# One product of the first layer made by seven inner products for pairs of units, in the last two of four sequences

## The chip, the cores and the metric

The kernel runs on one core of one Trainium2 chip. The metric is the time of one execution on the device in microseconds (us), as a median of three runs.

## The reference

Four sequences of 768 tokens go through an attention block with eight heads of 64, in which a query sees only the keys of its own cluster, and then through a feed-forward block. The change is in the feed-forward block alone, which is, for the attention's output `x` of 768 x 512 a sequence:

```python
mu = np.mean(x, axis=-1, keepdims=True)
var = np.mean((x - mu) ** 2, axis=-1, keepdims=True)
xn = (x - mu) / np.sqrt(var + 1e-06) * g_ln
ch = np.maximum(xn @ w_ch1, 0.0) @ w_ch2      # 512 x 2048, 2048 x 512
return (x + ch).astype(np.float32)
```

Everything is float32.

## The kernel before

**Stages.** The attention of all sequences comes first (0 to about 316 us of the span). Then each sequence b = 0 to 3 has a first layer (`xn @ w_ch1` and the ReLU) and a second layer. From sequence 1 on the second layer is `deep_layer`. The span's stages are, roughly: first layer of sequence 0 to 388 us and its second layer to 466; then a first layer and a second layer each for sequence 1 (466 to 604), 2 (604 to 740) and 3 (740 to 881).

**The first layer.** It is one step of a Strassen scheme in Winograd's form: the weight `w1` is taken as 2 x 2 blocks (two halves of the 2048 hidden rows, two halves of the 512 inputs), the tokens as 2 x 2 blocks (two halves of the inputs, two halves of the tokens), and seven block products replace eight. The block products are cut into eight units j = 0 to 7 of 128 hidden rows of each half (`NFH` = 8). `first_layer(b, j, part)` makes product `part` of unit j: `product` (L853) issues two matmuls, one for each 128 inputs of a half, with 128 x 128 weights and 384 columns (`HC`), into one PSUM bank. Products 1, 6, 7 and 4 add up in one bank `x`, 5 and 3 in a bank `z`; product 2 (`w1_block(0, 1, j)` with `x_block(b, 1, 0)`) has a bank `y` of its own. Six banks serve x and z in turn, two serve y and small things. In between, the contents of x are kept: ScalarE copies them (`kept`, L881) as p1 after product 1, u2 after 6, u3 after 7; VectorE adds p1 to y, u2 and u3 to z (`add_relu`, L886), and ScalarE takes the ReLU in place (`relu`, L894) or straight from x (L922). A product that adds onto x waits until the copy of what was in it is done.

The operands that aren't given blocks are sums by VectorE: four of the tokens a sequence (`x_sum`, L645) and four of the weights a unit (`w1_sums`, L661, made one unit ahead).

**The second layer.** `deep_layer` is two steps of the same scheme: 7 x 7 products, each of four matmuls with 192 columns (`QC`), `deep_product` (L1150), with VectorE's and ScalarE's adds and copies of 192 columns (L1163, L1165). Its weights, or sums of them, come from DRAM through a ring of ten places (`ring_load`, L1092); its other operands are sums of the hidden tiles: `outer_sums` (L1103 to L1106, a unit at a time, while the first layer runs), `outer_late`, `inner_sums` (L1124, L1126, quarters) and `inner_late` (L1131, L1133). The first product's quarter sums for chunks 0 to 2 of four stand in the last unit of the first layer, those of the last chunk after it.

**What sets the order.** In these stages the order of the instructions on TensorE, VectorE, ScalarE and SP queue is the order in which the Python code issues them; each engine takes its own in that order and waits by semaphores. `first_units(b, j)` issues a unit: products 1, 2, 4 (of unit j - 1), 6, 3 (of unit j - 1), 5, 7, with ReLUs, the next unit's weight sums and the outer sums of unit j - 1 in fixed places. `unit_end(b, j)` follows each unit: on ScalarE the row norm of one tile of the next sequence's tokens (`norm_rows`, L573 to L575, whose rows SP loads, L560), jobs that the second layer before put off with `later` (an add of the input, `add_rest`, L1203, and a transposition to the output's form, `turn`, L1209; `None` ends what one unit end takes), and `leave(4)`, four of the output DMAs (L1223) that a transposition left behind, eight for each.

For sequences 2 and 3 the first layer's start is interleaved with the end of the second layer before: product 1 of unit 0 stands before the last step of `deep_layer`, and then come products 2, 6, 5, 7 of unit 0.

Of the kernel before, what the change touches and what calls it, by code (L numbers as in the profile page):

```python
# [23 lines left out]
def kernel(  # L24
# [1100 lines left out]
        if 1 in which:  # L1125
            nc.vector.tensor_tensor(a21[:, cs], a11[:, cs], a21[:, cs], ALU.subtract)  # L1126

    def inner_late(st, m, way):
        q = st["q", m]
        if way == 1:  # L1130
            nc.vector.tensor_tensor(q[6], q[5], q[1], ALU.subtract)  # L1131
        else:
            nc.vector.tensor_tensor(q[3], q[2], q[6], ALU.subtract)  # L1133

# [86 lines left out]
    def leave(n, queues=(nc.sync,)):  # L1221
        for i, (to, y) in enumerate(leaving[:n]):
            queues[i % len(queues)].dma_start(out=to, in_=y)  # L1223
        del leaving[:n]

    pending = []

# [3 lines left out]
    def deep_layer(b, more, st):  # L1231

        done = {}

        def ahead_of(m):
            p = st[m] = {}
            onto = {2: 1, 3: 5}.get(m)
            p["add"] = done.get(onto)
            p["to"] = done[m] = done[onto] if onto else unit(f"m{m}")
            if m == ORDER[-1] and not more:  # L1240
                p["ends"] = {}

        def sum_onto(i, j):
            nc.vector.tensor_tensor(done[i], done[i], done[j], ALU.add)

        def last_part(o, way):

            part = {2: (0, 0), 7: (1, 1), 4: (1, 0), 3: (0, 1)}.get(way)
            if part is None:
                return  # L1250
            r, j = part
            queues = (nc.sync, nc.scalar, nc.gpsimd, nc.gpsimd) if way == 7 else (nc.sync, nc.scalar)
            if way in (4, 3):

# [12 lines left out]
            y = unit("y_end")[:, 0, :QC]  # L1267
            nc.vector.transpose(y, o[:, j].rearrange("p (t a r) -> p t a r", a=2, r=Q)[:, :, r])
            to = out[b].rearrange("(a r t) m -> a (r t) m", r=Q, t=NT)[r]
            for i in range(P // Q):  # L1270
                m = MH + j * P + i * Q
                queues[i % len(queues)].dma_start(  # L1272
                    out=to[:, m : m + Q], in_=y[i * Q : (i + 1) * Q].rearrange("r (t f) -> r t f", f=Q)
                )

        def between():
            first_layer(b, NFH - 1, 3)
            relu(len(summed))
# [12 lines left out]

        def out_of(r, k, m):
            return lambda: turn(b, r, k, done[m])

        def onto(i, j):
            return lambda: sum_onto(i, j)

        jobs = {
            (4, 1): [lambda: first_layer(b, NFH - 1, 4)],
            (4, 2): [between],  # L1300
            (4, 5): [lambda: rest_load(b, 0)],
            (4, 3): [rest(1, 0, 4)],
            (7, 6): [s4(0)], (7, 4): [s4(1)], (7, 3): [s4(2)], (1, 6): [s4(3)],
            (1, 4): [onto(4, 7)], (6, 3): [onto(6, 1)],
            (5, 4): [onto(4, 6)], (5, 3): [onto(5, 6)], (2, 6): [onto(7, 5)],
        }
        for i, m in enumerate(ORDER[1:]):
            for n, way in enumerate((5, 7)):
                jobs.setdefault((ORDER[i], way), []).append(lambda m=m, n=n: inner_sums(st, m, (n,)))
        if more:  # L1310
            for at, (i, c) in (
                ((4, 4), (0, 0)), ((7, 5), (0, 1)), ((1, 3), (0, 2)), ((6, 6), (0, 3)),
                ((6, 5), (1, 0)), ((6, 4), (1, 1)), ((5, 6), (1, 2)), ((5, 5), (1, 3)),
            ):
                jobs.setdefault(at, []).append(norm(i, c))
            for at, c in (((4, 7), 1), ((7, 2), 2), ((7, 3), 3)):
                jobs.setdefault(at, []).append(lambda c=c: norm_load(b + 1, c))
            jobs[2, 4] = [out_of(1, 0, 4)]
            jobs[2, 3] = [rest(0, 0, 2), lambda: rest_load(b, 1)]
            jobs[3, 6] = [lambda: x_sum(b + 1, 1)]  # L1320
            jobs[3, 5] = [lambda: w1_sums(b + 1, 0, (0, 1))]
            jobs[3, 7] = [lambda: first_layer(b + 1, 0, 1)]
            jobs[3, 4] = [lambda: x_sum(b + 1, 2)]
            later(
                rest(1, 1, 7), out_of(1, 1, 7), out_of(0, 0, 2), None,
                rest(0, 1, 3), out_of(0, 1, 3), None,
            )
        else:
            jobs[7, 2] = [lambda: rest_load(b, 1)]
            jobs[1, 3] = [rest(1, 1, 7)]  # L1330
            jobs[5, 6] = [rest(0, 0, 1), onto(4, 6)]
            del jobs[5, 4]
            jobs[2, 5].append(rest(0, 1, 5))
            jobs[2, 1] = [out_of(1, 0, 4)]
            jobs[2, 7].append(out_of(1, 1, 7))
            jobs[2, 3] = [out_of(0, 0, 2)]

        for m, way in STEPS:
            if way == 1:
                ahead_of(m)  # L1340
            deep_product(st, m, way)
            ring_load(b)
            leave(2 if more else 4, (nc.sync,) if more else (nc.sync, nc.scalar))
            if way == 1:
                inner_late(st, m, way)
            for job in jobs.get((m, way), ()):
                job()
            if way == 2:
                inner_late(st, m, way)
            if m == 3 and not more:  # L1350
                for part in {4: (), 3: (4, 3)}.get(way, (way,)):
                    last_part(done[m], part)
        leave(len(leaving))
        places[1, 1], places["e"] = places["e"], places[1, 1]

    deep = {}

    def first_units(b, j):

        chunks = within.pop(j, []) if b == 0 else []  # L1360
        for part, ahead in ((1, 0), (2, 0), (4, 1), (6, 0), (3, 1), (5, 0), (7, 0)):
            if chunks and part in (1, 3):
                split_weight(chunks[0])
            if j >= ahead:
                first_layer(b, j - ahead, part)
            if part in (4, 6, 3):
                relu(1)
            if chunks and part in (2, 3):
                m = chunks.pop(0)
                join_weight(m)  # L1370
                load_weight(m + RAWS)

            if part == 5 and j + 1 < NFH:
                w1_sums(b, j + 1)
            if part == 5 and b and j:
                outer_sums(j - 1, b > 1 or j > 4)
                if j + 1 == NFH:
                    inner_sums(deep[b], ORDER[0], cs=slice(0, NQH - 1))

    with tc.manual_schedule(engines=order):  # L1380
        first_layer(0, 0, 1)
# [79 lines left out]
    with tc.manual_schedule(engines=order | {mybir.EngineType.SP}):  # L1461
# [4 lines left out]
        def unit_end(b, j):  # L1466

            if b + 1 < B:
                if j == 0:
                    rows_load(b + 1, 1)  # L1470
                if j < NT:
                    norm_rows(b + 1, j)
            if b == 1:
                leave(4)
# [19 lines left out]
                norm_stats(b + 1)  # L1494
            if b + 1 < B and j + 2 == NFH:
                norm_stat_rows(b + 1)
            leave(4)
            if b == 1:
                if turning and j % 2 == 0:
                    columns_turn(row, lambda out, in_: leaving.append((out, in_)))  # L1500
# [7 lines left out]
        for b in range(1, B):  # L1508
            deep[b] = {}
            if b + 1 < B:  # L1510
                rows_load(b + 1, 0)
            if b == 1:
                w2_back(1)
                first_units(b, 0)
            else:
                first_layer(b, 0, 2)
                first_layer(b, 0, 6)
                relu(1)
                w1_sums(b, 0, (2, 3))
                x_sum(b, 3)  # L1520
                first_layer(b, 0, 5)
                first_layer(b, 0, 7)
                x_sum(b, 4)
                w1_sums(b, 1)
            unit_end(b, 0)
            for j in range(1, NFH):
                first_units(b, j)
                unit_end(b, j)
            relu(len(summed))
            inner_sums(deep[b], ORDER[0], cs=slice(NQH - 1, NQH))  # L1530
            if b == 1:
                first.close()
                units = pool("units", 1)
# [233 lines left out]
```

## Time and profile before

| | |
|---|---|
| median of three runs | 883.36 us (883.06 to 883.62) |
| the profiled execution | 882.89 us, span 881.1 us, granted TensorE clock 0.998 |
| TensorE matmul busy | 871.2 us, 99% of the span |
| VectorE busy | 703.9 us, 80% |
| ScalarE busy | 403.3 us, 46% |
| first layer of sequence 2, from 604 to 671 us | TensorE 67.0 us, VectorE 38.7, ScalarE 33.7 |
| first layer of sequence 3, from 740 to 807 us | TensorE 67.0 us, VectorE 38.7, ScalarE 24.2 |

The span is the time from the first to the last instruction of the profiled execution; its own time has about 1.8 us more. A float32 matmul leaves two records on TensorE. Records overlap, since matmuls are pipelined, so that a matmul's cost is read from the distance between starts and not from its duration. A group of instructions is named by its line in the kernel, its engine and its operation, then output and inputs by the names of the tiles.

### The profile page before, as it was taken

The numbers are of one execution on the slowest core, as the hardware profiler recorded it, in microseconds if no ns is written. First come the engines' busy times: TensorE is split into PE (matmuls) and PEld (weight loads), VectorE is DVE, ScalarE is ACT, GpSimd is POOL, SyncE is SP. The second block draws the span as 40 slices with busy tenths as digits, with TensorE's granted clock in tenths as the row PEclk, the third lists the DMA queues.
The fourth block names the chain that finished last, engine by engine and source line by source line (L and its number), as shares of the span: only waits on it lengthen the run. The fifth ranks groups of instructions, "written<-read, shape, count | busy, mean of one in ns | idle before, by whom it ended". The sixth has DMA issues, their size and how long they took to land.

```text
span 881.1 us, 13202 instructions
## 1 busy us (share of the span) xinstructions
PE 871.2 (99%) x4648; PEld 575.4 (65%) x4648; DVE 703.9 (80%) x1148; ACT 403.3 (46%) x742; POOL 77.9 (9%) x143
## 2 busy tenths in 40 slices
PE   9999999999999999999999999999999999999996
PEld 5444444444444445568886558997557997556996
DVE  6899999999999888959677787997546887645775
ACT  6777788888888823330004542102552101333110
POOL 1011221222222212110000000000000000000000
PEclk9999999999999999999999999999999999999999
DMA  7777899999986328876675888854236862511875
GB/s 155 145 128 128 147 178 186 206 194 203 186 184 188 100 83 221 239 183 234 186 191 162 240 282 295 295 164 99 55 75 202 280 199 54 102 71 34 272 196 113
DMA packets 250426, 151.01 MB, mean 171 GB/s; under 512 B 192096, under 2 KB 207984, under 8 KB 249328
## 3 DMA queue, kind: packets, MB, share of 16 engines
q1 hardware_dynamic: 219328, 130.80, 56.1%
q0 software_dynamic: 7776, 15.03, 8.9%
q10 hardware_dynamic: 23248, 4.25, 2.7%
q8 instruction: 39, 0.64, 0.3%
q14 instruction: 35, 0.29, 0.1%
HBM read 108.40 MB, written 33.25 MB: 161 GB/s over the span
## 4 chain that ended last, share of the span: by engine, by line
PE 99%; DVE 0%; ACT 0%; issue 0%; ACTq 0%
PE x_ps L855 19%; PE s_ps L401 18%; PE a_ps L413 14%; PE x_ps L1150 12%; PE z_ps L855 9%; PE z_ps L1150 6%; PE x_ps L963 5%; PE y_ps L855 5%; PE y_ps L1150 3%; PE z_ps L963 2%; PE sim_ps L320 1%; PE den_ps L469 1%; PE y_ps L963 1%; PE idle_ps L700 0%; PE qk_ps L303 0%
## 5 line engine op out<-in xcount | busy, mean ns | idle before, releaser
L401 PE MATMUL s_ps<-t,t 64*128 64x384 f32 x768 | 154.8, 483 | 0.0
L401 PEld LDWEIGHTS s_ps<-t,t 64*128 64x128 f32 x768 | 68.0, 187 | 39.0 <-issue 38.3
L1150 PE MATMUL x_ps<-lower,w 128*128 128x192 f32 x448 | 80.8, 326 | 0.4 <-DVE u L1165 0.4
L1150 PEld LDWEIGHTS x_ps<-lower,w 128*128 128x128 f32 x448 | 74.2, 190 | 2.1 <-DVE u L1165 0.7
L886 DVE TENSOR_TENSOR lower<-z_ps,u 128x384 f32<-128x384 f32 x56 | 30.9, 553 | 52.7 <-PE z_ps L855 42.6
L396 ACT ACTIVATE e<-s_ps 128x768 f32<-128x768 f32 x84 | 67.1, 812 | 7.0 <-PE s_ps L401 6.4
L396 ACT ACTIVATE w<-s_ps 128x768 f32<-128x768 f32 x80 | 64.4, 812 | 8.3 <-PE s_ps L401 7.7
L894 ACT ACTIVATE lower<-lower 128x384 f32<-128x384 f32 x88 | 44.9, 521 | 43.7 <-DVE lower L886 43.7
L401 PE MATMUL s_ps<-mask,mask 64*128 64x384 bf16 x384 | 62.8, 323 | 1.0 <-ACT e L396 0.6
L881 ACT COPY u<-x_ps 128x384 f32<-128x384 f32 x64 | 30.6, 478 | 68.1 <-PE x_ps L855 68.0
L413 PE MATMUL a_ps<-e,v_sb 128*64 128x384 f32 x336 | 57.6, 488 | 0.0
L413 PE MATMUL a_ps<-w,v_sb 128*64 128x384 f32 x320 | 55.2, 488 | 0.0
L881 ACT COPY p<-x_ps 128x384 f32<-128x384 f32 x32 | 15.1, 472 | 83.7 <-PE x_ps L855 82.1
L855 PE MATMUL x_ps<-xn,w 128*128 128x384 f32 x128 | 46.6, 487 | 0.0
L855 PE MATMUL x_ps<-xn,ws 128*128 128x384 f32 x128 | 46.6, 487 | 0.0
L855 PE MATMUL x_ps<-xt,ws 128*128 128x384 f32 x128 | 46.6, 487 | 0.0
L855 PE MATMUL x_ps<-xt,w 128*128 128x384 f32 x128 | 46.5, 486 | 0.0
L855 PE MATMUL z_ps<-xn,ws 128*128 128x384 f32 x128 | 46.5, 486 | 0.0
L855 PE MATMUL y_ps<-xn,w 128*128 128x384 f32 x128 | 46.5, 486 | 0.0
L855 PE MATMUL z_ps<-xt,ws 128*128 128x384 f32 x128 | 46.5, 486 | 0.0
L413 PEld LDWEIGHTS a_ps<-e,v_sb 128*64 128x64 f32 x336 | 23.5, 137 | 31.8 <-issue 29.3
L1272 POOL DMA_DIRECT2D out_dram<-y_end x2 | 1.2, 597 | 485.4 <-DMA out_dram<-y 485.4
(232 smaller groups left out, 1678.6 us busy)
## 6 DMA issues: line engine op xcount, KB each, us to landing
w<-w_d SPq DMA_DIRECT2D x84, 256.0 KB, 3.1
raw<-in_moe_w_ch_dram SPq DMA_DIRECT2D x32, 512.0 KB, 4.8
w<-w_t SPq DMA_DIRECT2D x36, 256.0 KB, 5.1
w<-tb POOLq DMA_DIRECT2D x32, 256.0 KB, 5.6
w_d<-wt SPq DMA_DIRECT2D x7, 1024.0 KB, 5.6
w<-w_all SPq DMA_DIRECT2D x27, 256.0 KB, 2.9
v_sb<-in_v_dram SPq DMA_DIRECT2D x32, 192.0 KB, 4.4
xr<-x_d SPq DMA_DIRECT2D x24, 256.0 KB, 3.0
```

The source lines that it names most:

```text
L320: nc.tensor.matmul(sim[r : r + Q, :HC], cT[:, pr, :, :].rearrange("p j c -> p (j c)"), prepared[n][side][:, g * HC : (g + 1) * HC], start= ...
L396: nc.scalar.activation(e, s[:, :, :HC], AF.Exp, scale=SCALE)
L401: nc.tensor.matmul(s[:, j, :HC], of_keys[:, keys], of_queries[:, o : o + HC], start=part == first, stop=part != first, skip_group_check=True,)
L413: nc.tensor.matmul(acc[j * D : (j + 1) * D, :HC], loaded[n]["v"][:, j, c, :], e[:, j, :], start=(c == 0), stop=(c == NT - 1),)
L469: nc.tensor.matmul(den[r : r + Q, :HC], ones, sums[n, g][h][:, j, :], start=h == 0, stop=h == parts - 1, tile_position=(0, r), skip_group_ ...
L855: nc.tensor.matmul(bank[:, :HC], lhs[:, c, :], rhs[:, c], start=first and c == 0, stop=c == NDH - 1, skip_group_check=True,)
L881: nc.scalar.copy(t, bank[:, :HC])
L886: nc.vector.tensor_tensor(h, bank[:, :HC], other, ALU.add)
L894: nc.scalar.activation(h, h, AF.Relu)
L963: nc.tensor.matmul(bank[:, :MH].rearrange("p (h f) -> p h f", h=2), hidden[lhs + (c,)][:, tt * P : (tt + 1) * P], rhs[:, :, c], start=firs ...
L1150: nc.tensor.matmul(bank, w[:, c, :], a[:, c], start=way in (1, 2, 5) and c == 0, stop=c == NQH - 1, skip_group_check=True,)
L1272: queues[i % len(queues)].dma_start(out=to[:, m : m + Q], in_=y[i * Q : (i + 1) * Q].rearrange("r (t f) -> r t f", f=Q))
```

## The change

For sequences b >= `PAIRED` (2 and 3) product 2 is no longer issued. For each pair of units (j, j + 1, j even) the four block products that it stood for (two units, two groups of 128 inputs) are taken as a 2 x 2 block product with halves of 192 columns, and made by seven inner products of one matmul each (128 x 128 weights, 192 columns), by the same scheme. Inner products 1, 6, 7, 4 add up in one x bank, 5 and 3 in a z bank, 2 has a y bank. After 1, 6, 7 and 4 VectorE reads the bank and adds the unit's p1 (a half of it), then adds what it kept to y and z: seven adds of 192 columns a pair, in place of two of 384. The operands are four sums of tokens a sequence (`inner_x`, L1240 of the changed kernel) and four sums of 128 x 128 weights a pair (`inner_w`, L1254); the matmul is at L1272, the adds at L1276 to L1284. The ReLU of the tiles is as before.

The order changes with it. In these sequences a unit issues products 1, 5, 4, 6, 3, 7, with the inner products of a pair spread over its two units, and product 6 follows product 1 of unit 0 at the start. The row norm moves from the unit's end to after product 1, the outer sums to other places in the unit, the put-off jobs by one unit end, eight output DMAs leave at a unit's end instead of four, and the first quarter sums of the second layer all stand after the last unit, their late sum in two pieces (`inner_late` with `cs`).

```diff
+    def inner_x(b):
+        x = x_block(b, 1, 0)
+        (b11, b12), (b21, b22) = [[x[:, k, h * NT // 2 : (h + 1) * NT // 2] for h in range(2)] for k in range(2)]
...
+        for o, x, y in ((t1, b12, b11), (t2, b22, t1), (t3, b22, b12), (t4, b21, t2)):
+            nc.vector.tensor_tensor(o, x, y, ALU.subtract)
+        inner[b, "x"] = {1: b11, 2: b21, 3: b22, 4: t4, 5: t1, 6: t2, 7: t3}
+
+    def inner_w(b, j):
+        (a11, a12), (a21, a22) = [[w1_block(0, 1, j + i)[:, k] for k in range(2)] for i in range(2)]
...
+        for o, x, op, y in (
+            (s1, a21, ALU.add, a22), (s2, s1, ALU.subtract, a11),
+            (s3, a11, ALU.subtract, a21), (s4, a12, ALU.subtract, s2),
+        ):
+            nc.vector.tensor_tensor(o, x, y, op)
+        inner[b, "w"] = {1: a11, 2: a12, 3: s4, 4: a22, 5: s1, 6: s2, 7: s3}
+
+    def inner_products(b, j, ways):
+        a, x, kept = inner[b, "w"], inner[b, "x"], inner[b, "kept"]
+        half = [slice(h * QC, (h + 1) * QC) for h in range(2)]
+        p1, u2, u3 = [kept[:, i * QC : (i + 1) * QC] for i in range(3)]
+        add = {1: (0, 0), 6: (0, 1), 7: (1, 1), 4: (1, 0)}
...
+        for way in ways:
+            name = {2: "y", 5: "z", 3: "z"}.get(way, "x")
+            if way in (1, 2, 5):
+                inner[b, "in", name] = ps(name + "_ps")
+            bank = inner[b, "in", name][:, :QC]
+            nc.tensor.matmul(bank, a[way], x[way], start=way in (1, 2, 5), stop=True, skip_group_check=True)
+            if way in add:
+                r, h = add[way]
+                o = {1: p1, 6: u2, 7: u3}.get(way)
+                nc.vector.tensor_tensor(
+                    to(r, h) if o is None else o, bank, sets[b, j + r]["p1"][:, half[h]], ALU.add
+                )
+            if way == 2:
+                nc.vector.tensor_tensor(to(0, 0), bank, p1, ALU.add)
+            elif way == 7:
+                nc.vector.tensor_tensor(to(1, 1), inner[b, "in", "z"][:, :QC], u3, ALU.add)
+            elif way == 3:
+                nc.vector.tensor_tensor(to(0, 1), bank, u2, ALU.add)
+                summed.extend(hidden_tile(0, j + i) for i in range(2))
...
-            jobs[3, 6] = [lambda: x_sum(b + 1, 1)]
+            jobs[3, 6] = [lambda: x_sum(b + 1, 1), lambda: x_sum(b + 1, 2)]
...
-            jobs[3, 4] = [lambda: x_sum(b + 1, 2)]
             later(
-                rest(1, 1, 7), out_of(1, 1, 7), out_of(0, 0, 2), None,
+                *[None] * (b + 1 >= PAIRED), rest(1, 1, 7), out_of(1, 1, 7), out_of(0, 0, 2), None, *[None] * (b + 1 >= PAIRED),
...
-            if way == 1:
+            if way == 1 and b >= PAIRED and m == ORDER[0]:
+                for cs in (slice(0, NQH - 1), slice(NQH - 1, NQH)):
+                    if cs.start:
+                        inner_sums(st, m, cs=cs)
+                    inner_late(st, m, way, cs)
+            elif way == 1:
                 inner_late(st, m, way)
...
-        for part, ahead in ((1, 0), (2, 0), (4, 1), (6, 0), (3, 1), (5, 0), (7, 0)):
+        parts = ((1, 0), (2, 0), (4, 1), (6, 0), (3, 1), (5, 0), (7, 0))
+        sums_after, inner_at = 5, {}
+        if b >= PAIRED:
+            parts = ((1, 0), (5, 0), (4, 1), (6, 0), (3, 1), (7, 0))
+            sums_after, inner_at = 3, {5: (7,), 6: (4, 3)} if j % 2 else {6: (1, 2), 7: (6, 5)}
+            if j == 1:
+                inner_at = {1: (1, 2), 6: (6, 5), 3: (7,), 7: (4, 3)}
+        for part, ahead in parts:
...
+            if part in inner_at:
+                inner_products(b, j - j % 2, inner_at[part])
+                relu(len(summed))
+            if inner_at and part == 1 and j % 2 == 0:
+                if j == 2:
+                    outer_sums(0, True)
+                inner_w(b, j)
+            if inner_at and part == 1 and b + 1 < B and j < NT:
+                norm_rows(b + 1, j)
...
-            if part == 5 and j + 1 < NFH:
+            if part == sums_after and j + 1 < NFH:
                 w1_sums(b, j + 1)
...
+            if inner_at and part == 7 and j % 2 == 0:
+                outer_sums(j - 1, True)
...
-            leave(4)
+            leave(8 if b >= PAIRED else 4)
...
             else:
-                first_layer(b, 0, 2)
                 first_layer(b, 0, 6)
-                relu(1)
                 w1_sums(b, 0, (2, 3))
                 x_sum(b, 3)
                 first_layer(b, 0, 5)
+                x_sum(b, 4)
                 first_layer(b, 0, 7)
-                x_sum(b, 4)
                 w1_sums(b, 1)
+                inner_x(b)
+                inner_w(b, 0)
...
-            inner_sums(deep[b], ORDER[0], cs=slice(NQH - 1, NQH))
+            if b >= PAIRED:
+                inner_sums(deep[b], ORDER[0], cs=slice(0, NQH - 1))
+            else:
+                inner_sums(deep[b], ORDER[0], cs=slice(NQH - 1, NQH))
```

More of the change, by code (lines that the diff above doesn't have):

```diff
@@ L1126, in inner_sums, with inner_late @@
             nc.vector.tensor_tensor(a21[:, cs], a11[:, cs], a21[:, cs], ALU.subtract)
-    def inner_late(st, m, way):
+    def inner_late(st, m, way, cs=slice(0, NQH)):
         q = st["q", m]
         if way == 1:
-            nc.vector.tensor_tensor(q[6], q[5], q[1], ALU.subtract)
+            nc.vector.tensor_tensor(q[6][:, cs], q[5][:, cs], q[1][:, cs], ALU.subtract)
         else:
@@ L1224, in leave @@
         del leaving[:n]
+    PAIRED = 2
+    inner = {}
+    def inner_x(b):
+        x = x_block(b, 1, 0)
+        (b11, b12), (b21, b22) = [[x[:, k, h * NT // 2 : (h + 1) * NT // 2] for h in range(2)] for k in range(2)]
+        t1, t2, t3, t4 = [
+            unit_part.rearrange("p (t q) -> p t q", q=2 * Q)
+            for unit_part in unit("xi").rearrange("p a c -> p (a c)").rearrange("p (i c) -> i p c", i=4)
+        ]
+        for o, x, y in ((t1, b12, b11), (t2, b22, t1), (t3, b22, b12), (t4, b21, t2)):
+            nc.vector.tensor_tensor(o, x, y, ALU.subtract)
+        inner[b, "x"] = {1: b11, 2: b21, 3: b22, 4: t4, 5: t1, 6: t2, 7: t3}
@@ new lines, in inner_w @@
+    def inner_w(b, j):
+        (a11, a12), (a21, a22) = [[w1_block(0, 1, j + i)[:, k] for k in range(2)] for i in range(2)]
+        if (b, "s") not in inner:
+            inner[b, "s"] = unit("wi").rearrange("p a c -> p (a c)")
+            inner[b, "kept"] = unit("pi").rearrange("p a c -> p (a c)")
+        s1, s2, s3, s4 = [inner[b, "s"][:, i * P : (i + 1) * P] for i in range(4)]
+        for o, x, op, y in (
[4 more added lines that the diff above has]
+        inner[b, "w"] = {1: a11, 2: a12, 3: s4, 4: a22, 5: s1, 6: s2, 7: s3}
@@ new lines, in inner_products, with to @@
+    def inner_products(b, j, ways):
[3 more added lines that the diff above has]
+        add = {1: (0, 0), 6: (0, 1), 7: (1, 1), 4: (1, 0)}
+        def to(r, h):
+            return hidden_tile(0, j + r)[:, half[h]]
+        for way in ways:
[17 more added lines that the diff above has]
+                summed.extend(hidden_tile(0, j + i) for i in range(2))
@@ L1371, in first_units @@
                 load_weight(m + RAWS)
-            if part == 5 and j + 1 < NFH:
+            if part == sums_after and j + 1 < NFH:
                 w1_sums(b, j + 1)
-            if part == 5 and b and j:
-                outer_sums(j - 1, b > 1 or j > 4)
-                if j + 1 == NFH:
+            if part == sums_after and b and j:
+                if not inner_at or j % 2 and j > 1:
+                    outer_sums(j - 1, b > 1 or j > 4)
+                if j + 1 == NFH and not inner_at:
                     inner_sums(deep[b], ORDER[0], cs=slice(0, NQH - 1))
+            if inner_at and part == 7 and j % 2 == 0:
+                outer_sums(j - 1, True)
     with tc.manual_schedule(engines=order):
@@ L1468, in unit_end @@
             if b + 1 < B:
-                if j == 0:
+                if j == 0 and b < PAIRED:
                     rows_load(b + 1, 1)
-                if j < NT:
+                if j < NT and (b < PAIRED or j == 0):
                     norm_rows(b + 1, j)
@@ L1511 @@
                 rows_load(b + 1, 0)
+                if b >= PAIRED:
+                    rows_load(b + 1, 1)
             if b == 1:
@@ L1529 @@
             relu(len(summed))
-            inner_sums(deep[b], ORDER[0], cs=slice(NQH - 1, NQH))
+            if b >= PAIRED:
+                inner_sums(deep[b], ORDER[0], cs=slice(0, NQH - 1))
+            else:
+                inner_sums(deep[b], ORDER[0], cs=slice(NQH - 1, NQH))
             if b == 1:
```

## The prediction

> **What bounds the kernel now.** I read the page's busy table and the 40 slices first, then the tensor engine's timeline in the first layer of sequence 2 (604 to 671 us), then the vector engine's and the groups by form.
>
> ```profile
> span 881.1 us, 13202 instructions
> PE 871.2 (99%) x4648; PEld 575.4 (65%) x4648; DVE 703.9 (80%) x1148; ACT 403.3 (46%) x742; POOL 77.9 (9%) x143
> PE   9999999999999999999999999999999999999996
> ```
>
> TensorE is busy in every slice but the last, so a microsecond of tensor work taken out is a microsecond of time, as long as nothing else makes it wait. The timeline gives the price of a product, as the distance between starts (durations overlap):
>
> ```profile
> 664.17 1.45 PE L855 MATMUL x_ps<-xt,w 128*128 128x384 f32 x4
> 665.46 1.45 PE L855 MATMUL x_ps<-xt,ws 128*128 128x384 f32 x4
> 666.75 1.45 PE L855 MATMUL z_ps<-xn,ws 128*128 128x384 f32 x4
> 668.04 1.45 PE L855 MATMUL z_ps<-xt,ws 128*128 128x384 f32 x4
> ...
> 677.10 1.46 PE L1150 MATMUL z_ps<-qs,w 128*128 128x192 f32 x8
> 678.40 1.46 PE L1150 MATMUL x_ps<-fifth,w 128*128 128x192 f32 x8
> ```
>
> A product of the first layer, two matmuls of 384 columns (four records, each float32 matmul leaves two), takes 1.29 us: 0.645 a matmul. A product of the second layer is four matmuls of 192 columns, each with weights of its own, and takes 1.30 us: 0.325 a matmul, all but exactly half. A unit of seven products takes 9.03 us (616.33 to 625.36).
>
> Vector work in one whole unit of that stage, and the spare time:
>
> ```profile
> 643.40:652.40 9.00, 9.00 (x29) 5.32 (x28) 4.48 (x11) 4.81 (x12) 0.00 (x0) 1.00 0.56 140
> ```
>
> The columns after the length are PE, PEld, DVE, ACT, POOL busy, the clock (full), DMA share and GB/s. VectorE works 4.48 us of 9.00, ScalarE 4.81.
>
> **What it removes and adds on TensorE.** In sequences 2 and 3 product 2 goes from all 16 units: 16 x 1.29 = 20.64 us. Each of 8 pairs of units gets seven single matmuls of 192 columns: 56 x 0.325 = 18.20 us. The changed program's instruction order shows just this, and no other tensor work changed. Saved: 2.44 us, 0.305 a pair. The nearest row for the new matmuls is the second layer's: the same width, and there too every matmul has new weights and every product changes bank. I take it. From above I bound a matmul by its LDWEIGHTS record (190 ns, for two passes 0.38 us): 56 x 0.38 = 21.28, a loss of 0.64 us. From below by half of a 384-column one (0.3225): a gain of 2.58.
>
> A rule speaks against cutting products this small: the Trainium skill, "TensorE: Matmul & The Clock Gate", section "Back-to-back issue gap", says that in a stream of weight load and matmul both set the spacing, and gives about 81 ns at 128 columns where the streaming alone would be 56. By that ratio, as an estimate from the page, a new matmul would cost 0.47 us and the change would lose about 5.7 us. The 1.30 us row above shows no such addition at 192 columns, so the row stands.
>
> **What it adds on VectorE, and whether that stays hidden.** The groups by form (time in all, mean ns of one), and then three starts from VectorE's timeline:
>
> ```profile
> L886 DVE TENSOR_TENSOR lower<-y_ps,p 128x384 f32<-128x384 f32 x32 | 17.4, 544 | 14.2 <-PE y_ps L855 14.1 <-ACT p L881 0.2
> L1165 DVE TENSOR_TENSOR u<-x_ps,m 128x192 f32<-128x192 f32 x12 | 4.2, 352 | 4.1 <-PE x_ps L1150 4.1
> L1124 DVE TENSOR_TENSOR qs<-lower 128x192 f32<-128x192 f32 x2 | 0.7, 358 | 1.2 <-ACT lower L894 1.2
> ```
>
> ```profile
> 625.27 0.40 DVE L661 TENSOR_TENSOR ws<-w 128x256 f32<-128x256 f32 x1
> 625.71 0.42 DVE L661 TENSOR_TENSOR ws<-ws,w 128x256 f32<-128x256 f32 x1
> 626.05 0.42 DVE L661 TENSOR_TENSOR ws<-w 128x256 f32<-128x256 f32 x1
> ```
>
> Per pair two adds of 384 go (2 x 0.544 = 1.09 us); seven of 192 come (7 x 0.352 = 2.46) and four of 128 columns on weights. No row has 128 columns: the slope from 256 (0.418) to 192 (0.358) puts it at 0.30; bounds 0.2 and 0.358; I take 0.29. That is +2.53 us a pair, and 4 x 0.358 a sequence for the tokens: 23 us in all. With it VectorE works 2 x 4.48 + 2.53 = 11.5 of the 17.76 us of a pair. The sum fits; what matters is that four of the new matmuls must wait until VectorE has read the bank they write, or has made their operand. So I go through the queues by hand. Rules from rows: a reader starts 0.20 us after its product (product 3 ends at 666.75 + 1.29 = 668.04, the add starts at 668.24); an instruction that reads the one ahead starts 0.03 after its end (625.27 + 0.40, 625.71), another one 0.08 before it (625.71 + 0.42, 626.05).
>
> The first pair is the tightest. Zero is the end of product 7 of unit 0. TensorE: product 1 of unit 1 to 1.29, inner 1 and 2 to 1.94, product 5 from 1.94, 4 from 3.23, 6 from 4.52, inner 6 at 5.81 and 5, product 3 of unit 0 from 6.46, inner 7 at 7.75, product 7 from 8.08, inner 4 at 9.37 and 3 at 9.69. VectorE: ScalarE has copied u3 at 0.68, the add starts at 0.71, the first weight sum ends at 1.18 + 0.42 = 1.60 (needed at 1.94: room 0.34). Three more weight sums, four token sums and four inner weight sums bring the read of inner 1 to 4.83, done at 5.18 (needed at 5.81: room 0.63). Product 3 ends at 7.75; its add starts at 7.95, the read of inner 7 at 8.42, done at 8.77 (needed at 9.37: room 0.60); the add that frees z ends at 9.15 (needed at 9.69: room 0.54). So no wait. That small rooms do cost nothing, the trace shows: the sum that product 7 of unit 0 reads ended at 604.83 + 0.95 = 605.78, and the product started on schedule at 606.00.
>
> In later pairs 2.6 to 2.9 us of other products lie between an inner product and the one waiting for its read, so rooms are larger. The worst queue there is the jobs that `later` puts off (an add of 0.95 and two transpositions of 0.95) ahead of pair 2. On the same axis unit 1's adds keep VectorE until 11.55, the jobs until 14.32, three outer sums (1.53 in the trace) until 15.85, four inner weight sums until 16.80; the read of inner 1 is done at 17.15, needed at 18.41: room 1.26.
>
> What is moved: product 6 of unit 0 takes product 2's place, so token sum 2 is made under the last products of the second layer: it follows sum 1 (596.12 + 0.95), and the weight sums behind it end near 598.85, 3.3 us before product 6, now at 602.13. The read behind these, at 598.44 in the trace, slips to about 598.8 and ends at 599.16; TensorE's step at 599.53 waits for it: room 0.37. At the entry of the second layer the quarter sums now stand behind the last unit: counted from the start of its first product, the outer sums of unit 6 take VectorE until 1.56, the last unit's add until 2.03, two quarter sums until 3.6, the late sum of three chunks ends at 4.40, needed at 5.18; the fourth chunk's ends at 5.46, needed at 6.16. Rooms 0.7 to 0.8. ScalarE's row norm (five records, 1.80 us from 607.87 to 609.67) moves from the unit's end behind the copy of p1: on the axis above from 1.97 to 3.8, and ScalarE is next needed for product 4's output at 4.72. Eight output DMAs leave at a unit's end where four did; behind them on SP queue the row loads (asked two units ahead of ScalarE's use) and the ring's weight loads (wanted only in the second layer). I cost all this at nothing; were the cover gone, each missed joint would cost its overrun in each of two sequences.
>
> **The sum.** The profiled execution took 882.89 us (span 881.1): 882.89 - 2.44 = 880.45. The three runs' median, 883.36, lies 0.47 above it, so I forecast 883.36 - 2.44 = 880.92, 880.9 us. That is 0.28%; no change, to a measurement of this kernel, is within 0.2% (1.77 us).
>
> **Rivals.**
> First, slower: a wait of VectorE gets in the way of the reads. The trace has one in this very stage:
>
> ```profile
> 623.46 0.98 DVE L1209 STREAM_TRANSPOSE y<-m 128x768 f32<-128x768 f32 x1 [4.61 <-DMA out_dram<-y]
> ```
>
> There the third transposition waits for a buffer that leaves in two portions of four DMAs at two unit ends; TensorE's unit took 9.03 us all the same. If one of 4.61 us stood ahead of pair 2's read, all above the room of 1.26 would stop TensorE: 3.35 us a sequence, 6.7 in two, 887.6 us. Slower by over 0.2% it is once it costs 2.44 + 1.77 = 4.21 us, 2.1 a sequence: from a stall of 1.26 + 2.1 = 3.4 us on. Against it: the first two transpositions now come a unit later, long after their buffers' DMAs, and eight DMAs leave at once (8 x 0.65 us to issue, about 2.1 to land), a unit and more before the third.
>
> Second, the same: single 192-column matmuls between 384-column ones don't hide their weight loads; at 0.38 us each 883.36 + 0.64 = 884.0. For it, they stand alone or in twos; against it, the 1.30 us.
>
> Third, a partial gain: VectorE's small sums or latencies are slightly longer and the first pair misses some of four rooms by 0.2 to 0.5 us each, 0.7 to 1.6 us over two sequences: 881.6 to 882.5. That the product isn't replaced is excluded by the instruction order.
>
> **How the numbers follow.** Forecast 0.79, first rival 0.06, second 0.06, partial gain 0.09 (of which a third still over 0.2% faster). Faster 0.79 + 0.03 = 0.82; same 0.12; slower 0.06. Range: below, the 2.58 us gain and the spread of three runs (0.3) give 880.4, rounded to 880.3; above, the partial gain's end, 882.5. Outside lie the two costly rivals, 0.12.
>
> **What would show it.** Right: a pair of units takes 17.76 us between starts of product 1, against 18.06; the seven inner matmuls show 0.33 us between starts; TensorE has no idle before them; VectorE busy rises by some 23 us. Wrong: idle at inner 4, 3 or 6 put down to VectorE (first or third rival), or starts of 0.38 us and more (second).

## The result and the profile after

The changed kernel takes 880.0 us, median of seven runs (879.66 to 881.18), against 883.24 us for the kernel before in seven runs beside it (882.47 to 883.86): a ratio of 0.9965, 95% interval [0.9954, 0.9977]. It is faster, as forecast, by more than the 0.2% that counts as a difference here. But 880.0 lies 0.3 us under the low end of the range, so the range failed.

The busy table of the changed kernel and TensorE's 40 slices:

```profile
span 878.1 us, 13380 instructions
PE 867.9 (99%) x4696; PEld 581.1 (66%) x4696; DVE 723.4 (82%) x1230; ACT 404.5 (46%) x742; POOL 78.0 (9%) x143
PE   8999999999999999999999999999999999999996
```

TensorE is still busy throughout (8 tenths in the first slice, where it had 9), with 3.3 us less of work recorded; VectorE works 19.5 us more. The timeline of TensorE over unit 1 of sequence 2, in which the first pair's inner products stand (start, record's length, line, tiles):

```profile
605.71 1.45 PE L855 MATMUL x_ps<-xn,w 128*128 128x384 f32 x4
607.00 0.49 PE L1272 MATMUL x_ps<-xn,w 128*128 128x192 f32 x2
607.32 0.49 PE L1272 MATMUL y_ps<-xn,w 128*128 128x192 f32 x2
607.65 1.45 PE L855 MATMUL z_ps<-xt,ws 128*128 128x384 f32 x4
...
610.23 1.45 PE L855 MATMUL x_ps<-xt,ws 128*128 128x384 f32 x4
611.52 0.49 PE L1272 MATMUL x_ps<-xi,wi 128*128 128x192 f32 x2
611.84 0.49 PE L1272 MATMUL z_ps<-xi,wi 128*128 128x192 f32 x2
612.17 1.45 PE L855 MATMUL z_ps<-xn,ws 128*128 128x384 f32 x4
...
615.40 0.49 PE L1272 MATMUL z_ps<-xn,wi 128*128 128x192 f32 x2
615.72 1.45 PE L855 MATMUL x_ps<-xn,w 128*128 128x384 f32 x4
```

Read the starts: 607.00, 607.32, 607.65 are 0.32 to 0.33 us apart, the price taken from the second layer. No line carries a wait in brackets, and from product 1 of unit 1 (605.71) to that of unit 2 (615.72) it is 10.01 us, what the hand count on its axis gave. From there to product 1 of unit 4 (633.48) a pair of units takes 17.76 us, the time forecast. The groups by form say the same for all matmuls of a kind (busy in all, mean ns of one, then idle just before them):

```profile
L1272 PE MATMUL x_ps<-xi,wi 128*128 128x192 f32 x32 | 7.8, 326 | 0.0
L1276 DVE TENSOR_TENSOR pi<-x_ps,p 128x192 f32<-128x192 f32 x24 | 8.5, 353 | 8.8 <-PE x_ps L1272 8.7
L1254 DVE TENSOR_TENSOR wi<-w 128x128 f32<-128x128 f32 x16 | 4.4, 277 | 0.0
```

TensorE idles 0.0 us before the inner products; it is VectorE that waits for them (8.7 us), not the other way round.

Where did the 3 us between the two spans come from? The traces can be cut at fixed points: product 1 of the first unit of sequence 2, the first product of each second layer, and the last transposition on TensorE, before and then after:

```profile
874.40 0.40 PE L1259 MATMUL turned<-ident,end 128*96 128x128 f32 x2 [0.46 <-ACT y_end L1261]
```

```profile
871.66 0.39 PE L1320 MATMUL turned<-ident,end 128*96 128x128 f32 x2 [0.46 <-ACT y_end L1322]
```

Between the first and the last of these points lies all code that the change touches, apart from token sum 2 and the transfers.

| us | before | after |
|---|---|---|
| start of sequence 2's product 1 | 598.24 | 597.95 |
| from there to its second layer | 72.38 | 71.15 |
| sequence 3, product 1 to second layer | 72.26 | 71.04 |
| product 1 of sequence 2 to the last transposition | 276.16 | 273.71 |
| from there to the end of the span | 6.70 | 6.44 |

The two first layers gain 1.23 and 1.22 us, 2.45 in all, against 2.44 forecast. The other 0.55 us (0.29 ahead of the first point, 0.26 behind the last) are in code that the change leaves alone. Part of it can be seen at the start of sequence 0's first layer, before and then after:

```profile
319.89 1.45 PE L855 MATMUL y_ps<-xn,w 128*128 128x384 f32 x4
321.30 1.56 PE L855 MATMUL x_ps<-xt,ws 128*128 128x384 f32 x4
322.70 1.45 PE L855 MATMUL z_ps<-xt,ws 128*128 128x384 f32 x4
```

```profile
319.82 1.45 PE L855 MATMUL y_ps<-xn,w 128*128 128x384 f32 x4
321.11 1.45 PE L855 MATMUL x_ps<-xt,ws 128*128 128x384 f32 x4
322.40 1.45 PE L855 MATMUL z_ps<-xt,ws 128*128 128x384 f32 x4
```

The same three products start 1.41 and 1.40 us apart in the one execution and 1.29 apart in the other. That raised the question whether this belongs to the change or to the execution, which the first two runs settle.

### The profile page after: what moved, and what is told of

It is laid out like the page before. It is cut to its first block, busy times and chain, and to the rows that moved or that the text cites. A ratio compares the mean times of both kernels' runs of the same rounds, so it can differ in the third digit from the quotient of the medians.

```text
span 878.1 us, 13380 instructions
## 1 busy us (share of the span) xinstructions
PE 867.9 (99%) x4696; PEld 581.1 (66%) x4696; DVE 723.4 (82%) x1230; ACT 404.5 (46%) x742; POOL 78.0 (9%) x143
## 4 chain that ended last, share of the span: by engine, by line
PE 97%; DMA 1%; SPq 0%; DVE 0%; ACT 0%; ACTq 0%; issue 0%; DVEq 0%
PE x_ps L855 19%; PE s_ps L401 17%; PE a_ps L413 14%; PE x_ps L1150 12%; PE z_ps L855 9%; PE z_ps L1150 6%; PE x_ps L963 5%; PE y_ps L1150 3%; PE z_ps L963 2%; PE y_ps L855 2%; PE den_ps L469 1%; PE sim_ps L320 1%; PE x_ps L1272 1%; PE y_ps L963 1%; PE z_ps L1272 1%; SPq L92 0%
## 5 line engine op out<-in xcount | busy, mean ns | idle before, releaser
L413 PEld LDWEIGHTS a_ps<-w,v_sb 128*64 128x64 f32 x320 | 22.4, 137 | 30.4 <-issue 27.6
```

The lines of the kernel that those rows point to most:

```text
L413: nc.tensor.matmul(acc[j * D : (j + 1) * D, :HC], loaded[n]["v"][:, j, c, :], e[:, j, :], start=(c == 0), stop=(c == NT - 1),)
```

## The experiments

All share the kernel before on their chip as the yardstick. The theory: TensorE sets the pace; the change is worth the columns it takes out (2.44 us), nothing else in it is worth or costs anything, as long as VectorE's reads come within their rooms; what the first comparison showed beyond it is scatter. The rivals: the moved transfers and the new order bring the rest; or the inner products cost more than counted and something else brings more.

### The same two kernels again

No edit to either kernel.

> The kernel before once more, unchanged. It asks how far two executions of one program differ outside the changed stretch, since the changed kernel's profile gained 2.45 us between product 1 of sequence 2 and the last transposition on TensorE, and 0.55 us elsewhere (0.29 by 390 us of the span, 0.26 after TensorE's last instruction). If the 0.55 us is scatter: the time is that of the kernel before within 0.2%, and this profile differs from the first profile of before by 0.2 to 0.4 us in those two places as well. If it belongs to the change: this profile repeats the first one within 0.1 us in both places (TensorE reaches the first second-layer product of sequence 0 near 389.5 us, and 6.7 us lie behind its last instruction).

> The changed kernel once more. If the gain is TensorE's work alone: 2.45 us, a ratio of 0.9972, and the sequences 2 and 3 give 1.23 us each in the profile. If something else in the change brings 0.6 us: 3.0 to 3.2 us, 0.9965, and the places outside the changed stretch are again 0.2 to 0.3 us shorter than in the profiles of before.

Measured: the kernel before once more 883.82 us against 883.6 (29 runs, 882.61 to 884.96), ratio 1.0004 [0.9995, 1.0013]. The changed kernel 880.88 us (880.43 to 881.84), ratio 0.9972 [0.9961, 0.9984]; the forecast was 880.9 and 2.44/883.36 makes a ratio of 0.9972.

Between the fixed points the second pair of traces repeats the first to a hundredth: 276.16 us for the kernel before, 273.71 for the changed one. Outside them it does not: sequence 2's product 1 starts at 599.30 and 598.82, the tail is 6.94 and 6.87. One program differs from itself by 1.06 us there (598.24 and 599.30, the kernel before), and the two executions of the changed kernel by 1.30 us in both places together (spans of 878.1 and 879.4). So the 2.45 us belong to the change, and the 0.55 us of the first pair to those two executions. What makes the executions differ stays open.

### The new order alone

```diff
-                inner_products(b, j - j % 2, inner_at[part])
+                even = j - j % 2
+                for way, unit_of in ((1, even), (7, even + 1)):
+                    if way in inner_at[part]:
+                        first_layer(b, unit_of, 2)
...
```

Product 2 of each unit stands where inner product 1 or 7 of the pair stood, and the inner sums are gone; order, row norms, put-off jobs, eight DMAs at a unit's end and the split late sum stay as in the changed kernel.

> The changed order (products, row norms, outer sums, put-off jobs, DMAs in eights, quarter sums) with product 2 kept whole, two matmuls of 384 columns a unit, and no inner sums or products. If only the inner products gain: the time of the kernel before, 0 within 0.3 us, no wait on TensorE in sequences 2 and 3. If the order or the DMAs bring part of the gain: 0.5 to 0.8 us less than before, ratio 0.9991 to 0.9994.

Measured: 883.27 us, ratio 0.9997 [0.9988, 1.0006]; 276.15 us between the fixed points, against 276.16. The new order and the moved transfers bring nothing and cost nothing. The whole gain is the inner products'.

### In one sequence only

```diff
-    PAIRED = 2
+    PAIRED = 3
...
```

Sequence 2 starts with products 1, 2, 6, 5, 7 of unit 0 again, without inner sums.

> The inner products and their order in sequence 3 alone. If the gain is TensorE's work: half of it, 1.22 us (0.9986), with 0 in sequence 2 and 1.22 in sequence 3 of the profile. If a fixed part comes from the tail, which this kernel shares: 1.22 + 0.3 to 0.6 = 1.5 to 1.8 us.

Measured: 882.05 us, ratio 0.9986 [0.9977, 0.9995], half of the gain within the interval. The trace is sharper: sequence 2's first layer takes 72.37 us, as before, and sequence 3's 71.04, as after. The gain is local to the layer in which the product is replaced, 1.22 us each.

### Filling a small room

After `inner_w(b, 0)`, ahead of the read of inner product 1, VectorE makes two sums of 128 x 768 that nothing uses.

```diff
+                for _ in range(2):
+                    spare = xpool.tile([P, S], F32, tag="row", name="spare", bufs=2)
+                    nc.vector.tensor_tensor(spare, normed[b][0][:, 0], normed[b][0][:, 0], ALU.add)
```

> The changed kernel with two further sums of 128x768 on VectorE (0.87 us each from start to start) behind the inner weight sums of the first pair, in sequences 2 and 3; their output is used by nothing. The hand count has 0.63 us of room before inner product 6 of that pair. If the count of rooms is right: the read of inner 1 ends at 6.92 instead of 5.18 on its axis, TensorE waits 1.1 us before inner 6 in each of the two sequences and nowhere else, 2.2 us over the changed kernel, 883.1. If TensorE has more cover than counted (banks to go on with): 0 to 1 us over. If VectorE's load counts as such and not the place: 3.5 us over, twice 2 x 0.87.

Measured: 883.33 us, ratio 0.9996 [0.9986, 1.0006]: the gain is gone. TensorE's waits from 597 to 860 us (total, number, longest), of which the changed kernel has none, and the place in the timeline:

```profile
PE x_ps L1272 <- DVE pi L1276: 1.9, 2, 1.0
```

```profile
607.17 1.45 PE L855 MATMUL x_ps<-xn,w 128*128 128x384 f32 x4
...
611.70 1.45 PE L855 MATMUL x_ps<-xt,ws 128*128 128x384 f32 x4
614.10 0.59 PE L1272 MATMUL x_ps<-xi,wi 128*128 128x192 f32 x2 [0.95 <-DVE pi L1276]
614.53 0.49 PE L1272 MATMUL z_ps<-xi,wi 128*128 128x192 f32 x2
```

Two waits, one a sequence, both before inner product 6 of the first pair and nowhere else. The joints behind it aren't tested by this: once TensorE is late, they are due later too. VectorE's read of inner 1, in the changed kernel and then in this run:

```profile
610.49 0.35 DVE L1276 TENSOR_TENSOR pi<-x_ps,p 128x192 f32<-128x192 f32 x1
```

```profile
613.70 0.35 DVE L1276 TENSOR_TENSOR pi<-x_ps,p 128x192 f32<-128x192 f32 x1
```

The room can be read from it. Counted from product 1 of unit 1, the read starts after 6.53 us (613.70 - 607.17), where it was 4.78 in the changed kernel (610.49 - 605.71): 1.75 us of new work. Inner 6 was due 1.29 after product 6, at 612.99, and starts at 614.10, 1.11 late. The room was 1.75 - 1.11 = 0.64 us; the hand count said 0.63. The next matmul then starts 0.43 after inner 6 instead of 0.325, so that a late joint costs 0.11 us beyond the delay: 1.22 a sequence, which is what the fixed points show (72.38 and 72.26 us, again as before).

### The put-off jobs where they were

```diff
-                *[None] * (b + 1 >= PAIRED), rest(1, 1, 7), out_of(1, 1, 7), out_of(0, 0, 2), None, *[None] * (b + 1 >= PAIRED),
+                rest(1, 1, 7), out_of(1, 1, 7), out_of(0, 0, 2), None,
...
-            leave(8 if b >= PAIRED else 4)
+            leave(4)
```

> The changed kernel with the put-off jobs one unit end earlier, as before, and four output DMAs at a unit's end instead of eight. If a wait of VectorE ahead of the reads costs TensorE what exceeds the room: an add and two transpositions (2.8 us) stand ahead of the read of inner 1 of the first pair, less the room of 0.63 gives 2.1 us a sequence before inner 6, 4.3 us in all, and if the third transposition waits for its buffer again (4.6 us before) some 2 to 3 us more a sequence before inner 6 of the second pair: 4.3 to 10 us over the changed kernel, so slower than before. If these moves are idle: 0.

Measured: 886.65 us, ratio 1.0041 [1.0025, 1.0057]: slower than the kernel before. VectorE's and then TensorE's timeline in sequence 2:

```profile
610.85 0.95 DVE L1203 TENSOR_TENSOR m<-m,rest_x 128x768 f32<-128x768 f32 x1
611.84 1.84 DVE L1209 STREAM_TRANSPOSE y<-m 128x768 f32<-128x768 f32 x2
613.60 0.32 DVE L1276 TENSOR_TENSOR pi<-x_ps,p 128x192 f32<-128x192 f32 x1
```

```profile
613.97 0.59 PE L1272 MATMUL x_ps<-xi,wi 128*128 128x192 f32 x2 [1.93 <-DVE pi L1276]
614.40 0.49 PE L1272 MATMUL z_ps<-xi,wi 128*128 128x192 f32 x2
614.73 2.56 PE L855 MATMUL z_ps<-xn,ws 128*128 128x384 f32 x4
617.08 0.85 PE L1272 MATMUL x_ps<-xi,wi 128*128 128x192 f32 x2
```

The add and two transpositions (610.85 to 613.60, 2.75 us) stand ahead of the read that inner product 6 needs; less the room of 0.64 it is 2.11 us late, and it starts 2.09 after it was due (610.59 + 1.29 = 611.88). This is the first rival's mechanism, a VectorE job ahead of a read, at another joint than the rival named; the wait for a buffer's DMAs, from which the rival took its price, does not occur in this trace. Two edits were undone at once, but since VectorE waits for no DMA in the first layers of sequences 2 and 3, it is the jobs' place that costs, not the four DMAs in place of eight. So the few words with `None` in the change are needed: without them the product's replacement loses.

But 2.2 us a sequence (delay and late restart) is not all. Sequence 3's first layer takes 73.24 us, 2.20 over the changed kernel's; sequence 2's takes 75.04, 3.89 over. The 1.69 us more are in the last timeline: product 3 (614.73) takes 2.35 us to the next start where 1.29 is usual. The windows name the cause (the columns after the length are PE, PEld, DVE, ACT, POOL busy, then the granted clock, DMA share and GB/s):

```profile
612.00:614.00 2.00, 0.07 (x2) 0.03 (x1) 1.92 (x3) 0.48 (x1) 0.00 (x0) 1.00 0.01 4
614.00:616.00 2.00, 2.00 (x7) 1.45 (x8) 0.72 (x2) 0.00 (x0) 0.00 (x0) 0.73 0.47 74
616.00:618.00 2.00, 2.00 (x6) 1.40 (x5) 0.56 (x1) 0.08 (x1) 0.00 (x0) 0.50 0.69 164
618.00:620.00 2.00, 2.00 (x9) 1.31 (x9) 1.90 (x6) 0.92 (x2) 0.00 (x0) 0.92 0.58 91
```

After the idle stretch the granted clock goes to 0.50 and is back by 620. What the clock lacks in the last three rows, 2.00 x (0.27 + 0.50 + 0.08), is 1.70 us, all of the 1.69. The same wait of 1.93 us in sequence 3 is not followed by it.

### A sequence with less room

The inner products also in sequence 1, in whose first layer VectorE is busy 52.05 of 64.80 us (469.8 to 534.6) in the kernel before, against 39.70 of 71.20 in sequence 2.

```diff
+    FROM = 1
...
-        if b >= PAIRED:
+        if b >= FROM:
             parts = ((1, 0), (5, 0), (4, 1), (6, 0), (3, 1), (7, 0))
...
-                    outer_sums(0, True)
+                    outer_sums(0, b > 1)
```

The inner sums of sequence 1 lie in another pool, for which one buffer of the split weights is given up; unit 0 issues products 1, 6, 5, 7, and the row norms stay at the unit's end.

> The inner products in sequence 1 as well (with one buffer instead of two for the split second-layer weights, to make room). If only TensorE's work counts: 1.22 us less than the changed kernel, 879.2. If VectorE's load sets the limit: in sequence 1 VectorE worked 52.05 of 64.80 us of units 1 to 7, the change adds about 4 x 2.53 + 1.4 = 11.5 us to it, 63.6 us in 63.6, so that nothing is left for waits: TensorE idles before inner products of sequence 1, 3 to 10 us over the changed kernel.

Measured: 900.03 us, ratio 1.0193 [1.0176, 1.021], a loss of some 19 us to the changed kernel and more than expected. TensorE's long waits in sequence 1:

```profile
481.88 1.01 PE L1279 MATMUL x_ps<-xi,wi 128*128 128x192 f32 x2 [5.29 <-DVE pi L1283]
507.99 0.66 PE L1279 MATMUL x_ps<-xi,w 128*128 128x192 f32 x2 [3.57 <-DVE pi L1283]
530.24 0.59 PE L1279 MATMUL x_ps<-xi,w 128*128 128x192 f32 x2 [2.49 <-DVE pi L1283]
549.68 0.59 PE L1279 MATMUL x_ps<-xi,w 128*128 128x192 f32 x2 [1.24 <-DVE pi L1283]
```

These are 12.6 us, all before an inner product that waits for a read of VectorE. VectorE's load as such doesn't explain them: in sequence 1's first layer it is busy 63.5 of 88.5 us. Ahead of the first read it does other work for 6.1 us (475.40 to 481.51): fourteen small instructions, four sums for the second layer's weights, a transposition. Ahead of the second and third stands such work too, and in it VectorE itself waits for DMAs, 3.0 and 2.2 us. Of these, 1.53 and 0.30 us are for the DMA that empties the one buffer left of the split weights, a wait that the kernel before, with two, doesn't have; so a part of the loss comes with the experiment and not with the inner products. What TensorE's waits did to the clock comes on top:

```profile
482.00:488.00 6.00, 6.00 (x13) 4.18 (x14) 2.30 (x7) 0.52 (x1) 0.00 (x0) 0.51 0.40 152
508.00:512.00 4.00, 4.00 (x9) 2.66 (x10) 1.07 (x4) 0.94 (x2) 0.00 (x0) 0.57 0.25 95
```

Ten microseconds at about half clock lose some 5 us more; with the 12.6 that is most of the 19. The 2.49 us wait left the clock at 1.00 (530 to 534). That the change begins at sequence 2 has a reason in this arrangement; another order in sequence 1, or one with both buffers, was not tried.

### Narrower matmuls

Each inner product in two matmuls, of 128 and of 64 columns, with the same weights.

```diff
-            nc.tensor.matmul(bank, a[way], x[way], start=way in (1, 2, 5), stop=True, skip_group_check=True)
+            for lo, hi in ((0, 2), (2, 3)):
+                nc.tensor.matmul(
+                    bank[:, lo * 2 * Q : hi * 2 * Q], a[way], x[way][:, lo:hi],
+                    start=way in (1, 2, 5) and lo == 0, stop=True, skip_group_check=True,
+                )
```

> Each inner matmul of the changed kernel as two, of 128 and 64 columns, with the same weights: 112 matmuls for 56, the same columns in all. If a matmul's price goes by its columns (0.325 us at 192): 0.215 + 0.11, no change within 0.5 us. If the weight load sets the price of the smaller ones (its record lasts 190 ns in each of two passes): 0.38 us at most for each, 0.76 for a product in place of 0.325, up to 24 us over; with 0.21 us for 64 columns, about 6 us over.

Measured: 887.96 us, ratio 1.0051 [1.0035, 1.0068]. Between the fixed points 280.48 us, 6.77 over the changed kernel, 0.121 for each of the 56 inner products.

```profile
608.57 0.56 PE L1273 MATMUL x_ps<-xn,w 128*128 128x128 f32 x4
608.96 0.61 PE L1273 MATMUL y_ps<-xn,w 128*128 128x128 f32 x4
609.41 1.51 PE L855 MATMUL z_ps<-xt,ws 128*128 128x384 f32 x4
```

```profile
608.91 0.53 PEld L1273 LDWEIGHTS y_ps<-xn,w 128*128 128x128 f32 x4
609.36 0.95 PEld L855 LDWEIGHTS z_ps<-xt,ws 128*128 128x128 f32 x4
```

An inner product takes 0.39 and 0.45 us between starts, for the same 192 columns that took 0.325. (The view names the form of the wider part alone; x4 are the records of both.) Every part loads its weights again, in two passes: the second view has the four loads of one product, which take 0.45 us from the first to the next product's first, 0.11 us a load, although the record of one lasts 0.19. Four loads at 0.11 make 0.445 us, the 0.121 over 0.325 that was measured. So the second rival's mechanism is there, at 0.22 us a matmul and not at 0.38, and 192 columns (0.325) are above it. The Trainium skill's rule, "TensorE: Matmul & The Clock Gate", section "Back-to-back issue gap", that weight load and matmul together set the spacing of matmuls in a stream, agrees with these starts; at 192 float32 columns no start shows it.

## Why the prediction was right or wrong

**The range failed, the mechanism did not.** The step that failed is the low end of the range: "below, the 2.58 us gain and the spread of three runs (0.3) give 880.4, rounded to 880.3". The spread of three runs was taken for the scatter of a median, and it is too small. (The terms give 883.36 - 2.58 - 0.3 = 880.48; the 880.4 and the rounding added 0.2 us to them, and even that was not enough.) The medians of the kernel before were 883.24, 883.6, 883.82 and 883.78 in four sets of runs, its single runs 882.47 to 885.37; those of the changed kernel 880.0 and 880.88. A median of seven runs moved by 0.88 us between two comparisons. With about 1 us in place of 0.3 the low end would have stood at 879.8, and 880.0 inside. By the same scatter it is luck that the second comparison, 880.88, meets the forecast to 0.02 us; the 2.45 us between the fixed points are not luck, as four traces have them. The same mistake in small is the offset of 0.47 us between the profiled execution and the median: it was treated as a constant, but the profiled execution after was 879.91, 0.09 under its median.

**TensorE's sum** held: 2.44 us on record, 2.45 between the fixed points in both pairs of traces, and the first comparison's interval (0.9954 to 0.9977) contains 0.9972. Taking the second layer's row and not the bounds or the page's ratio (0.47 us, a loss of 5.7 us) was the choice that decided the sign: the split to 128 and 64 columns shows what that loss looks like when it is there. The upper bound of 0.38 us, two weight load records, was too high: loads start 0.11 us apart there, so two of them take 0.22.

**VectorE's additions**, 23 us on record, are 23.7 by the durations in the two traces: the sums of 192 columns took 0.352 to 0.358 us, those of 128 columns 0.277 to 0.292 (0.29 taken). The busy time, which the prediction said would rise by some 23 us, rose by only 19.5, since durations of neighbours that don't depend on each other overlap by some 0.08 us and the busy time counts that once. By stage, kernel before and then changed kernel:

```profile
597.90:669.10 71.20, 71.20 (x233) 43.05 (x232) 39.70 (x84) 33.69 (x84) 0.00 (x0) 1.00 0.36 87
...
732.80:803.80 71.00, 71.00 (x235) 43.49 (x234) 40.12 (x84) 23.86 (x51) 0.00 (x0) 1.00 0.29 70
```

```profile
597.90:669.10 71.20, 71.20 (x260) 46.75 (x258) 49.08 (x125) 34.84 (x84) 0.00 (x0) 1.00 0.37 90
...
732.80:803.80 71.00, 71.00 (x257) 46.64 (x257) 48.87 (x123) 25.03 (x52) 0.00 (x0) 1.00 0.28 67
```

VectorE is at 69% of the stage and TensorE at all of it. That share alone would have said nothing about the two experiments that lost: in the one with two more sums VectorE works less than 2 us more in a sequence, and the gain is gone.

**The rooms** held. The four of the first pair were counted at 0.34, 0.63, 0.60 and 0.54 us; from the end of VectorE's instruction to the matmul's start the changed kernel's trace has 0.35, 0.68, 0.59 and 0.53, and the room ahead of pair 2, counted at 1.26, is 1.27. Filled to overflowing, the second of these measured 0.64; there the matmul started 0.05 us after the read's end (614.05, 614.10). The smallest, before product 5 of unit 1, was not filled by any run. The last room at the entry of the second layer, counted at 0.7, is 0.57. The walk through the queues by hand was worth its length: it named the joint at which both later experiments waited, and gave their delays to within 0.1 us.

**The put-off jobs, the row norms and the output DMAs**, costed at nothing, cost nothing (the new order alone: 0.01 us between the fixed points). The stall of 4.61 us for output buffers, the first rival's ground, is not among the changed kernel's VectorE waits. Where the prediction was thin is what a missed joint costs: "its overrun in each of two sequences" leaves out the late restart (0.11 us) and the clock (1.69 us in one of two sequences).

## What to carry to other kernels

Where TensorE sets the pace, one more step of a fast scheme on a product is worth the columns it saves, as long as the matmuls stay wide enough to cover their weight loads, as 192 float32 columns did here and 64 did not; take the price from a row of the same width in the same trace. Count the room before each read that a product waits for, not the engine's share: here one joint had 0.64 us of room, and 1.75 us of further work ahead of it took the whole gain of 2.45 us. And a forecast of a quarter of a per cent needs the scatter of medians in its range: cut the traces at fixed points to see the change itself, and repeat the pair before explaining a remainder.

## What the runs showed of the hardware

Two things had not been expected. TensorE's granted clock fell to 0.50 after single waits of 1.93, 3.57 and 5.29 us, for 3.41, 3.41 and 6.83 us, but not after other waits of 0.95, 1.24, 1.93 and 2.49 us. The Trainium skill, "TensorE: Matmul & The Clock Gate", Part 1, puts the fall behind an idle window of about 3.4 us in a free-running count. The traces agree with the count, but the window need not be idle throughout. In each of the ten traces all changes of the clock lie whole multiples of 3.413 us apart (in the run with sequence 1, for example, the clock is back at 487.90 and falls again at 508.38, six of them later). When a trace is cut into steps of this length at its own changes, every step at full clock in which TensorE idles 1.93 us or more, the idle end of the program included, is followed by half clock, and none with 1.38 us or less is. The wait of 1.93 us in sequence 2 lies within one step (611.52 to 614.93); the same wait in sequence 3 is cut at 751.46 into 0.70 and 1.23 us, and the 2.49 us wait at 528.86 into 1.11 and 1.38. So a wait of some 2 us can cost the clock or not, by where it falls. This is read from the traces; no run was made to test it.

And a matmul that comes late by a wait takes 0.43 us to the next start instead of 0.325, with the clock at 1.00 (after waits of 0.95, 1.24, 1.93 and 2.49 us alike). After the 0.95 us its first weight load starts with it, at 614.10; in the changed kernel the load for the same matmul starts at 611.20, 0.32 us ahead of it. The 0.11 us more equal one load as read from the split columns; that this is the reason was not tested.
